# Routing matmuls widened to the full array, capacities added last, and a shorter first routing chain

## The chip, the cores and the metric

The kernel runs on one core of a Trainium2 chip. The metric is device time in microseconds of the core. The engines are named as in the profile: PE (TensorE matmuls; PEld are its weight loads), DVE (VectorE), ACT (ScalarE), POOL (GpSimd) and SP (SyncE, which issues DMAs).

## The reference

Three computations follow each other on 2304 tokens of width 512. Attention with 4 x 8 heads (sequence 576, head width 64) adds a softmax over a sequence averaged by four and a softmax over a band of width 7. A mixture of 8 experts routes each token to one expert with a capacity of 288 tokens, by a greedy walk over all token and expert pairs in order of their gate logit. A feed-forward network (512 to 2048 to 512) with g = h * tanh(softplus(h)) follows.

```python
x = _attn_ref(q, k, v)            # (2304, 512) after the reshape
logits = x @ w_gate               # (2304, 8)
for idx in np.argsort(-logits.flatten()):
    tok, e = idx // 8, idx % 8
    if assigned[tok] >= 0 or counts[e] >= 288: continue
    assigned[tok] = e; counts[e] += 1
for e in range(8):
    out[assigned == e] = np.maximum(x[assigned == e] @ w1[e], 0) @ w2[e]
h = out @ w_in; out = (h * np.tanh(softplus(h))) @ w_out
```

## The kernel before

Attention (class `Attn`, L57 to L310) works on 16 pairs of heads, three groups of three 64-token blocks each, and writes x transposed into `xT`. A list of operations sorted by hand-set keys (`TP`) gives the order in which they are written; a scheduler then orders each engine's queue. `rmm` (L241) multiplies a 128-token tile of `xT` with the identity and the gate weights into the PSUM tile `rp`, in two halves; `rxr` copies the rows out on ACT, `rlg` sums the logits on DVE into `L`, and `rst` stores the rows to DRAM. `rp` has one buffer of tag "rw", and from tile 15 on half of the calls take the one buffer of tag "pd".

The router (class `Router`, `phase` L394) finds in phase k the next expert that fills up, and its 288 tokens. A phase takes the maximum of the remaining logits per token (`m`), a one-hot of its expert (in `AO[:, 1]`, called OH; `AO[:, 0]`, called A, holds the tokens already given away), and an integer key whose digits are searched in five levels. A level (L441) compares a digit with 128 or 64 thresholds (`cmp`, DVE), counts by expert on PE (`cnt`: one matmul with the negative capacities, `nrem`, from one partition, then 18 with 8 weight columns, L455), turns the signs into a count `fl` (`jk`, DVE), sends it to all partitions by a matmul (the vote `j8`, L462, 9 rows), and takes the largest (`jb`). Then `full` marks the expert, `s8` and `sf` (L485 to L487) pick its tokens, two matmuls (`to`, 36 columns, copied to `ts`; and `pp`) number them, and `it` (18 matmuls with 3 weight columns) and `ip` (a transpose) give the index list `idx` for the gather (`gather`, L692, indirect DMAs on POOL's queue).

In phase 0 `busy` (L385) puts matmuls on constants (`idle`, 128 x 512) into the waits of the routing chain.

The order of stages is a list (L849): phases 0 and 1, then experts E0 to E7, then the FFN groups. While expert k runs, `bg()` (L950) steps routing phase k + 2, so that matmuls of the router stand between those of the expert. An expert (`expert`, L703) transposes its gathered rows (`xtp`, L713), multiplies them with w1 (`hp`, L756 in plain f32, two passes per matmul) and with w2 (`ya`). E1 to E5 also convert pieces of the FFN weights on DVE and ACT (`Narrow`). The FFN is `group` (L772).

Of the kernel before, what the change touches and what calls it, by code (L numbers as in the profile page):

```python
# [29 lines left out]
RPD = 15  # L30
# [26 lines left out]
class Attn:  # L57
# [183 lines left out]
    def rmm(self, t, half):  # L241


        rp = self.rp[t, half] = (self.p_pd.tile([128, 2, 136], F32, name="rp", tag="pd") if t >= RPD and (t + half) % 2
                                 else self.p_rw.tile([128, 2, 136], F32, name="rp", tag="rw"))
        for i in range(2):
            self.nc.tensor.matmul(rp[:, i], self.xT[:, 2 * half + i, 128 * (t % 9):128 * (t % 9) + 128], self.a['idg_sb'][:, 2 * half + i], start=True, stop=True)  # L247
# [17 lines left out]
    def emit(self, nar=None, rload=None):  # L265
# [54 lines left out]
def host_route():  # L320
# [7 lines left out]
    tri = np.zeros((128, 164), f)  # L328
    tri[:, 0:128] = np.triu(np.ones((128, 128), f))
    tri[0:36, 128:164] = np.triu(np.ones((36, 36), f), 1)  # L330

    eye = np.concatenate([np.vstack([np.eye(8) * v, np.ones((1, 8))]) for v in EYES], axis=1)
    return dict(rsmall=small, rthr=it.astype(ml_dtypes.bfloat16), rtri=tri.astype(np.float16), reye=eye.astype(np.float16))

class Router:
    def __init__(self, nc, tc, ctx, a):
# [5 lines left out]
        self.tri = c.tile([128, 164], F16, name="rtri")  # L342
# [51 lines left out]
    def phase(self, k):  # L394
# [9 lines left out]
        A, OH = self.AO[:, 0], self.AO[:, 1]  # L404
# [5 lines left out]
        if not last:  # L410
            m0, sg, key, E = F("m0"), F("sg", I32), F("key", I32), P2("E", BF16)
            dg = [F(f"dg{i}", I32) for i in range(len(SH))]

        for c0, c1 in FIRST if k == 0 else [(0, 18)]:
            c = slice(c0, c1)
            V.tensor_reduce(out=m[:, c], in_=L[:, c], op=ALU.max, axis=AX.X)
            if not last:
                V.tensor_scalar_add(m0[:, c], m[:, c], 0.0)
                mi = m0[:, c].bitcast(I32)
# [7 lines left out]
            if k:  # L427
                wm2 = F("wm2")
                V.scalar_tensor_tensor(out=wm2, in0=self.inact, scalar=100.0, in1=wm, op0=ALU.mult, op1=ALU.add)
            V.tensor_tensor(out=OH[:, c], in0=w2[:, c], in1=bc8((wm2 if k else wm)[:, c]), op=ALU.is_equal)  # L430
# [3 lines left out]
        if not last:  # L434
# [6 lines left out]
            for l, K in enumerate(KS):  # L441
# [18 lines left out]
                V.tensor_scalar(out=jk[:, 0:K], in0=cnt[:, 0:K], scalar1=0.0, scalar2=0.0, op0=ALU.is_ge, op1=ALU.add, accum_out=fl[0:8])  # L460
# [14 lines left out]
            V.tensor_scalar(out=full, in0=fw, scalar1=fm[:, 0:1], scalar2=None, op0=ALU.is_equal)  # L475
# [3 lines left out]
        else:  # L479
            V.tensor_scalar(out=full, in0=self.rem, scalar1=30000.0, scalar2=None, op0=ALU.is_lt)  # L480
# [40 lines left out]
        R = sm.tile([128, 18, 3], F16, name="R")  # L521
# [27 lines left out]
        if not last:  # L549
# [8 lines left out]
            V.tensor_tensor(out=A, in0=A, in1=ON, op=ALU.add)  # L558
# [3 lines left out]
            V.tensor_scalar_mul(self.nrem, self.rem[0:1], -1.0)  # L562
# [81 lines left out]
class FFN:  # L644
# [58 lines left out]
    def expert(self, k, rows, exi):  # L703
# [9 lines left out]
        for dc in range(4):  # L713
            t = ps['h'].tile([128, 288], F32, name="xtp", tag="h")
            for g in range(3):
                nc.tensor.transpose(t[:, 96 * g:96 * g + 96], rows[g][:, 128 * dc:128 * dc + 128], self.a['ident_sb'][0:96, 0:96])
            if plain:
                (nc.vector.tensor_copy if dc % 2 else nc.scalar.copy)(xh[:, dc], t)
            else:
                nc.scalar.copy(xh[:, dc], t)  # L720
                nc.vector.tensor_tensor(out=xl[:, dc], in0=t, in1=xh[:, dc].bitcast(F32), op=ALU.subtract)
# [166 lines left out]
def body(nc, tc, a):  # L888
    with ExitStack() as ctx:
# [20 lines left out]
        nar.hold = hold  # L910
        def after(ins):
# [57 lines left out]
```

## Time and profile before

| | |
|---|---|
| Median of three runs | 899.55 us (895.21, 899.55, 899.56) |
| Profiled execution, its span | 894.45 us, 892.7 us |
| PE busy | 868.1 us (97%), 6792 instructions |
| PE weight loads | 728.0 us (82%) |
| DVE busy | 665.1 us (75%), 1819 instructions |
| ACT, POOL busy | 462.4 us (52%), 142.7 us (16%) |
| Mean granted PE clock | 0.998 of full speed (2.4 GHz) |
| Chain that ended last, by engine | PE 74%, DVE 12%, ACT 7%, issue 2%, DMA 2% |

A busy PE is not a PE at its peak: matmuls are pipelined, and a matmul counts as busy until its modelled end, so what a matmul costs is read from the distance between starts. A share over the span mixes stages; the stages are told apart by windows below.

### The profile page before, as it was taken

How to read it: one execution, taken by the hardware profiler on the slowest of the kernel's cores; microseconds unless marked ns; L12 is line 12 of the kernel's file. 1: busy time of each engine (PE TensorE's matmuls, PEld its weight loads, DVE VectorE, ACT ScalarE, POOL GpSimd, SP SyncE). 2: the span in 40 equal slices, each digit the busy share in tenths (PEclk: the TensorE clock that was granted, in tenths of full speed). 3: DMA queues.
4: the chain of work that ended last, by engine and by line, in shares of the span. 5: the costliest groups of instructions: out<-in, count | busy, mean ns of one | idle time of the engine just before them, and what ended most of it. 6: DMA issues, size and time to landing. Idle time of an engine off the chain costs nothing.

```text
span 892.7 us, 18176 instructions
## 1 busy us (share of the span) xinstructions
PE 868.1 (97%) x6792; PEld 728.0 (82%) x6792; DVE 665.1 (75%) x1819; ACT 462.4 (52%) x1136; POOL 142.7 (16%) x203
## 2 busy tenths in 40 slices
PE   7999999999989999999999999999998999999995
PEld 4778876466767777788999999999998999999994
DVE  6999876657879898987664788888887565665655
ACT  4778774012323233244555776666666565555553
POOL 5654410101202010112001000000000011111101
PEclk9999999999999999999999999999999999999999
DMA  8866522335575464659643343433333143333312
GB/s 214 201 193 193 170 91 91 100 110 158 165 227 186 160 221 154 225 181 299 210 148 101 84 119 119 119 118 109 118 95 93 48 118 95 95 96 95 95 48 71
DMA packets 69851, 123.44 MB, mean 138 GB/s; under 512 B 8738, under 2 KB 35618, under 8 KB 69762
## 3 DMA queue, kind: packets, MB, share of 16 engines
q1 hardware_dynamic: 34146, 75.08, 27.0%
q0 software_dynamic: 21984, 28.32, 12.4%
q10 hardware_dynamic: 13632, 18.88, 6.2%
q8 instruction: 53, 0.87, 0.4%
q14 instruction: 36, 0.29, 0.1%
HBM read 98.65 MB, written 23.60 MB: 137 GB/s over the span
## 4 chain that ended last, share of the span: by engine, by line
PE 74%; DVE 12%; ACT 7%; issue 2%; DMA 2%; POOL 1%; SPq 0%; POOLq 0%; DVEq 0%; ACTq 0%
PE hp L756 11%; PE hm L680 5%; PE hm L681 5%; PE hm L679 5%; PE oa L681 5%; PE oa L679 5%; PE oa L680 5%; PE ya L679 4%; PE ya L680 3%; PE ya L681 3%; PE cnt L455 3%; PE ya L730 2%; PE pvl L221 2%; PE sp L181 2%; PE rp L247 2%
## 5 line engine op out<-in xcount | busy, mean ns | idle before, releaser
L679 PE MATMUL hm<-Yh,wM_sb 128*128 128x256 f32 x576 | 161.5, 280 | 2.4 <-issue 2.4
L680 PE MATMUL hm<-Yl,wM_sb 128*128 128x256 f32 x576 | 162.3, 282 | 0.0
L681 PE MATMUL hm<-Yh,wM_sb 128*128 128x256 f32 x576 | 162.3, 282 | 0.0
L756 PE MATMUL hp<-xh,w 128*128 128x288 f32 x384 | 116.0, 422 | 0.0
L679 PE MATMUL oa<-wM_sb,gh 128*128 128x512 f32 x288 | 112.7, 391 | 2.6 <-ACT gh L841 2.6
L679 PEld LDWEIGHTS hm<-Yh,wM_sb 128*128 128x128 f32 x576 | 108.9, 189 | 5.5 <-issue 2.8
L681 PE MATMUL oa<-wM_sb,gl 128*128 128x512 f32 x288 | 113.0, 392 | 0.0
L680 PE MATMUL oa<-wM_sb,gh 128*128 128x512 f32 x288 | 112.3, 390 | 0.0
L680 PEld LDWEIGHTS hm<-Yl,wM_sb 128*128 128x128 f32 x576 | 108.8, 189 | 2.8
L681 PEld LDWEIGHTS hm<-Yh,wM_sb 128*128 128x128 f32 x576 | 108.4, 188 | 0.0
L841 ACT CAST gh<-eu 128x512 fp32r<-128x512 f32 (+1 forms) x73 | 44.9, 615 | 111.0 <-DVE eu L838 111.0
L835 DVE SCALAR_TENSOR_TENSOR eu<-eu 128x512 f32<-128x512 f32 (+1 forms) x73 | 50.1, 686 | 63.6 <-ACT eu L834 63.3
L765 ACT ACTIVATE gh<-hp 128x288 fp32r<-128x288 f32 (+1 forms) x64 | 26.2, 410 | 101.8 <-PE hp L756 87.3
L842 DVE TENSOR_TENSOR gl<-eu,gh 128x512 fp32r<-128x512 f32 (+1 forms) x73 | 50.0, 685 | 36.2 <-ACT gh L841 36.0
L756 PEld LDWEIGHTS hp<-xh,w 128*128 128x128 f32 x384 | 65.5, 189 | 13.0
L679 PE MATMUL ya<-gh,wbh 128*128 128x288 f32 x224 | 73.0, 329 | 0.0
L680 PE MATMUL ya<-gl,wbh 128*128 128x288 f32 x224 | 68.1, 305 | 0.0
L681 PE MATMUL ya<-gh,wbl 128*128 128x288 f32 x224 | 67.4, 302 | 0.0
L832 ACT ACTIVATE eu<-eu,one_sb 128x512 f32<-128x512 f32 (+1 forms) x73 | 52.3, 716 | 27.8 <-DVE eu L831 27.4
L681 PEld LDWEIGHTS oa<-wM_sb,gl 128*128 128x128 f32 x288 | 54.0, 188 | 12.3 <-DVE gl L842 0.8
L679 PEld LDWEIGHTS oa<-wM_sb,gh 128*128 128x128 f32 x288 | 54.1, 188 | 12.2 <-ACT gh L841 3.4
L680 PEld LDWEIGHTS oa<-wM_sb,gh 128*128 128x128 f32 x288 | 54.1, 188 | 9.1
(188 smaller groups left out, 1895.9 us busy)
## 6 DMA issues: line engine op xcount, KB each, us to landing
n<-in_wM_dram SPq DMA_DIRECT2D x32, 512.0 KB
w<-in_wE_dram SPq DMA_DIRECT2D x56, 256.0 KB
w2r<-in_wE_dram SPq DMA_DIRECT2D x40, 256.0 KB
Yh<-y_dram POOLq DMA_DIRECT2D x18, 512.0 KB, 5.7
Yl<-y_dram POOLq DMA_DIRECT2D x18, 512.0 KB, 5.1
wraw<-in_wE_dram SPq DMA_DIRECT2D x16, 512.0 KB
vw<-in_vw_dram SPq DMA_DIRECT2D x16, 315.0 KB
kT<-in_kT_dram SPq DMA_DIRECT2D x16, 291.0 KB
```

The lines of the kernel that those rows point to most:

```text
L181: self.mm = self.nc.tensor.matmul(sp[r, u], q[r, 64 * n:64 * n + 64], k[r, 64 * n:64 * n + W], start=False, stop=u == 2)
L221: self.nc.tensor.matmul(op[c, u], vw[:, 3 * g + u, c], d['aT'][:, u, c], start=True, stop=True)
L455: ct = nc.tensor.matmul(cnt[:, 0:K], OH[:, c, :], cmp[c], start=False, stop=(c == 17))
L679: mm(out, lh, rh, start=first, stop=False)
L680: mm(out, lh, rl, start=False, stop=False)
L681: mm(out, ll, rh, start=False, stop=last)
L756: nc.tensor.matmul(hp, w1[:, 128 * dc:128 * dc + 128], xh[:, dc], start=dc == 0, stop=dc == 3)
L765: self.cast = nc.scalar.activation(out=hh[:, 0:288], in_=hp, func=AF.Relu)
L832: nc.scalar.activation(out=u, in_=e, func=AF.Square, bias=one)
L835: nc.vector.scalar_tensor_tensor(out=u, in0=u, scalar=1.0, in1=r, op0=ALU.add, op1=ALU.mult)
L841: self.cast = nc.scalar.copy(gh[:, 0:w], e)
L842: self.mark = nc.vector.tensor_tensor(out=gl[:, 0:w], in0=e, in1=gh[:, 0:w].bitcast(F32), op=ALU.subtract)
```

## The change

All router matmuls get more than 64 weight columns and more than 64 rows, by zeros around the data (`OHw`, `Rw`, `nrem`, `eyes`, `fl`); only the first 13 counts of phase 0 stay at 8 columns. The capacities are spread over 128 partitions and from phase 1 on added after the counts. The `to` matmul and its copy give way to a running sum on DVE (`run`), and the tokens already given away are kept as one number per token (`aid`), so that `s8`, `sf` and A go. The last two `rp` tiles take PSUM buffers of the attention's scores and transposes. `xtp` holds one gather group with four 96-column pieces instead of one piece of all groups.

```diff
 def rmm(self, t, half):
-        rp = self.rp[t, half] = (self.p_pd.tile(...) if t >= RPD and (t + half) % 2 else self.p_rw.tile(...))
+        pool, tag = (self.p_pd, "pd") if t >= RPD and (t + half) % 2 else (self.p_rw, "rw")
+        if t >= 16:
+            pool, tag = (self.p_sc, "sc") if t == 16 else (self.p_tr, "tr")
...
-                add(k + TP['rlg'], self.rlg, t, h)
+                add(k + (TP['rxr'] - 0.01 if t >= 16 else TP['rlg']), self.rlg, t, h)
...
-    tri[:, 0:128] = np.triu(np.ones((128, 128), f))
-    tri[0:36, 128:164] = np.triu(np.ones((36, 36), f), 1)
-    eye = np.concatenate([np.vstack([np.eye(8) * v, np.ones((1, 8))]) for v in EYES], axis=1)
+    tri = -np.tril(np.ones((128, 128), f), -1)
+    eye = np.concatenate([np.vstack([np.eye(8) * v, np.zeros((64, 8)), np.ones((1, 8))]) for v in EYES], axis=1)
...
-        self.AO = c.tile([128, 2, 18, 8], F16, name="rAO")
+        self.OHw = c.tile([128, 208], F16, name="rOH")
+        self.Rw = [c.tile([128, 123], F16, name=f"rR{i}") for i in range(2)]
+        self.aid = c.tile([128, 18], F32, name="raid")
-        self.nrem = c.tile([1, 8], F16, name="rnrem")
+        self.nrem = c.tile([128, 72], F16, name="rnrem")
...
-                V.tensor_scalar_add(m0[:, c], m[:, c], 0.0)
-                mi = m0[:, c].bitcast(I32)
+                mi = m[:, c].bitcast(I32)
...
-                cnt = self.psr.tile([8, 128], F32, name="cnt", tag="rt")
-                nc.tensor.matmul(cnt[:, 0:K], self.nrem, self.one[0:1, 0:K], start=True, stop=False)
+                cnt = self.psr.tile([72, 128], F32, name="cnt", tag="rt")
+                nr = lambda a, b: nc.tensor.matmul(cnt[:, 0:K], self.nrem, self.one[:, 0:K], start=a, stop=b)
+                if not k:
+                    nr(True, False)
                 for c in range(18):
-                    ct = nc.tensor.matmul(cnt[:, 0:K], OH[:, c, :], cmp[c], start=False, stop=(c == 17))
+                    mm = 8 if not (l or k) and c < FIRST[0][1] else 72
+                    ct = nc.tensor.matmul(cnt[0:mm, 0:K], self.OHw[:, 8 * c:8 * c + mm], cmp[c], start=(k > 0 and c == 0), stop=(k == 0 and c == 17))
+                if k:
+                    nr(False, True)
...
-                jm = nc.tensor.matmul(j8, fl.to_broadcast([9, 128]), self.eye[1 if end else KS[l + 1]], start=True, stop=True)
-                self.busy(k, 16 if end else 4, jm)
+                jm = nc.tensor.matmul(j8, fl.to_broadcast([73, 128]), self.eye[1 if end else KS[l + 1]], start=True, stop=True)
+                self.busy(k, 7 if end else 4, jm)
...
-        V.tensor_tensor(out=s8, in0=self.AO.rearrange("p h c e -> p (h c) e"), in1=row8(full, 36), op=ALU.mult)
-        V.tensor_reduce(out=sf.rearrange("p h c -> p (h c)"), in_=s8, op=ALU.max, axis=AX.X)
-            V.tensor_tensor(out=sel, in0=ge, in1=sf[:, 1:2].to_broadcast([128, 2, 18]), op=ALU.mult)
-            V.tensor_tensor(out=sel[:, 0], in0=sel[:, 0], in1=sf[:, 0], op=ALU.add)
+            V.scalar_tensor_tensor(out=sel, in0=own.unsqueeze(1).to_broadcast([128, 2, 18]), scalar=fm[:, 0:1], in1=ge, op0=ALU.is_equal, op1=ALU.mult)
+        V.scalar_tensor_tensor(out=sel[:, 0], in0=aid, scalar=fm[:, 0:1], in1=sel[:, 0], op0=ALU.is_equal, op1=ALU.add)
-        nc.tensor.matmul(to[0:n], s2, self.one, start=True, stop=True)
-        V.tensor_copy(ts[0:n], to[0:n])
+        V.tensor_tensor_scan(out=run[:, 0:n], data0=self.one[:, 0:n], data1=s2, initial=0.0, op0=ALU.mult, op1=ALU.add)
-        self.busy(k, 9, nc.tensor.matmul(pp[:, 0:n], ts[0:n], self.tri[0:n, 128:128 + n], start=False, stop=True))
+        self.busy(k, 9, nc.tensor.matmul(pp[:, 0:n], self.one, run[:, 0:n], start=False, stop=True))
...
-            nc.tensor.matmul(it, R[:, c, :], oa[c], start=(c == 0), stop=(c == 17))
+            nc.tensor.matmul(it, Rw[:, 3 * c:3 * c + 72], oa[c], start=(c == 0), stop=(c == 17))
-        self.busy(k, 18, nc.tensor.transpose(ip, ig, self.a['ident_sb'][0:3, 0:3]))
+        self.busy(k, 20, nc.tensor.matmul(ip, ig, self.a['ident_sb'][0:72, 0:3], start=True, stop=True))
...
-        for dc in range(4):
-            t = ps['h'].tile([128, 288], F32, name="xtp", tag="h")
-            for g in range(3):
-                nc.tensor.transpose(t[:, 96 * g:96 * g + 96], rows[g][:, 128 * dc:128 * dc + 128], ...)
-                (nc.vector.tensor_copy if dc % 2 else nc.scalar.copy)(xh[:, dc], t)
+        for g in range(3):
+            t = ps['h'].tile([128, 4, 96], F32, name="xtp", tag="h")
+            for dc in range(4):
+                tp = nc.tensor.transpose(t[:, dc], rows[g][:, 128 * dc:128 * dc + 128], ...)
+            if g < 2:
+                self.busy(k, 1 + g, tp)
+                (nc.vector.tensor_copy if g == 1 else nc.scalar.copy)(xh[:, :, q], t)
```

The scheduler writes other queues from this. Three places follow, each before and then changed; line numbers are those of the respective file.

PE at the end of attention, from the last attention output (`pvl`) to the router's first matmul; the numbers tell the `rp` tiles apart. Before:

```order
L221 MATMUL pvl_2800<-aT_2795,vw_2371 64x64 x5
L247 MATMUL rp_2827<-idg_sb_106,xT_105 128x136 [waits DVE_49]
L247 MATMUL rp_2812<-idg_sb_106,xT_105 128x136 [waits DVE_49]
L247 MATMUL rp_2812<-idg_sb_106,xT_105 128x136
L247 MATMUL rp_2827<-idg_sb_106,xT_105 128x136 [waits DVE_49]
L247 MATMUL rp_2820<-idg_sb_106,xT_105 128x136 [waits DVE_49]
L247 MATMUL rp_2820<-idg_sb_106,xT_105 128x136
L247 MATMUL rp_2834<-idg_sb_106,xT_105 128x136 [waits DVE_49]
L247 MATMUL rp_2834<-idg_sb_106,xT_105 128x136
```

Changed:

```order
L221 MATMUL pvl_2809<-aT_2804,vw_2378 64x64 x5
L249 MATMUL rp_2834<-idg_sb_113,xT_112 128x136
L249 MATMUL rp_2841<-idg_sb_113,xT_112 128x136 [waits PE_49]
L249 MATMUL rp_2821<-idg_sb_113,xT_112 128x136 [waits DVE_49]
L249 MATMUL rp_2821<-idg_sb_113,xT_112 128x136
L249 MATMUL rp_2834<-idg_sb_113,xT_112 128x136 [waits DVE_49]
L249 MATMUL rp_2841<-idg_sb_113,xT_112 128x136
L249 MATMUL rp_2827<-idg_sb_113,xT_112 128x136 [waits DVE_49]
L249 MATMUL rp_2827<-idg_sb_113,xT_112 128x136
```

Before, three tiles after the last `pvl` wait for DVE to release a buffer or to fill `xT`, the last being 2834; now 2834 and 2841 have buffers of their own, and of the two tiles that still share one, 2827 ends the list.

DVE in phase 0 after the last vote, from `full` on (`ON` is the one-hot of tokens above the cut, `e` and `exi` give the expert's number, `rinact` the tokens out of play). Before, up to the second `sel`; the copy of `to` and pz follow 8 and 13 rows later:

```order
L475 TENSOR_SCALAR full<-fw,fm 128x8
L504 TENSOR_TENSOR ON<-rAO,ge 128x144
L485 TENSOR_TENSOR s_3162<-rAO,full 128x288
L546 SCALAR_TENSOR_TENSOR e_3258,ex<-full,rsmall 128x8
L552 TENSOR_SCALAR nf<-full 128x8
L487 TENSOR_REDUCE sf<-s_3162 128x36
L548 CAST exi<-ex 1x1
L553 TENSOR_TENSOR L<-L,nf 128x144
L492 TENSOR_TENSOR sel<-ge,sf 128x36
L556 TENSOR_TENSOR rinact<-rinact,ge 128x18
L558 TENSOR_TENSOR rAO<-rAO,ON 128x144
L493 TENSOR_TENSOR sel<-sel,sf 128x18
```

Changed, up to `pz`:

```order
L510 TENSOR_SCALAR full<-fw,fm 128x8
L502 SCALAR_TENSOR_TENSOR sel<-wm,fm,ge 128x36
L513 TENSOR_TENSOR ON<-rOH,ge 128x144
L503 SCALAR_TENSOR_TENSOR sel<-raid,fm,sel 128x18
L556 SCALAR_TENSOR_TENSOR e_3248,ex<-full,rsmall 128x8
L562 TENSOR_SCALAR nf<-full 128x8
L506 SCALAR_TENSOR_TENSOR run<-ones_67,sel 128x36
L558 CAST exi<-ex 1x1
L563 TENSOR_TENSOR L<-L,nf 128x144
L516 TENSOR_TENSOR pz<-sel,pp 128x36
```

The product and maximum over both halves of `rAO` are gone, `run` stands where the path over `to` was, and no row of the next phase stands between `sel` and `pz`.

PE in E0, between two runs of counts of one search level (before phase 1, level 2 to 3). Before:

```order
L455 LDWEIGHTS rAO
L455 MATMUL cnt<-cmp,rAO 8x128
L756 MATMUL hp<-xh,w_3598 128x288
L462 LDWEIGHTS rfl_71
L462 MATMUL j_3369<-reye,rfl_71 128x8
L756 MATMUL hp<-xh,w_3643 128x288
L451 LDWEIGHTS rnrem
L451 MATMUL cnt<-ones_67,rnrem 8x64
L756 MATMUL hp<-xh,w_3643 128x288 x2
L455 LDWEIGHTS rAO
L455 MATMUL cnt<-cmp,rAO 8x64
```

Changed:

```order
L465 LDWEIGHTS rOH
L465 MATMUL cnt<-cmp,rOH 72x128
L458 LDWEIGHTS rnrem
L458 MATMUL cnt<-ones_67,rnrem 72x128
L771 MATMUL hp<-xh,w_3584 128x288
L474 LDWEIGHTS rfl_71
L474 MATMUL j_3359<-reye,rfl_71 128x8
L771 MATMUL hp<-xh,w_3584 128x288
L771 MATMUL hp<-xh,w_3627 128x288 x2
L465 LDWEIGHTS rOH
L465 MATMUL cnt<-cmp,rOH 72x64
```

The capacity matmul (`rnrem`) left its place between the hp matmuls and stands at the end of the counts; the number of hp matmuls between vote and counts is the same.

## Rows read from the trace of the kernel before

**Rows 1.** Table by stages: length, busy of PE, PEld, DVE, ACT, POOL; clock, DMA.
```profile
0.00:146.60 146.60, 140.91 (x1821) 108.97 (x1821) 121.27 (x455) 105.08 (x497) 60.08 (x93) 1.00 0.59 162
...
182.00:224.10 42.10, 42.10 (x296) 27.31 (x295) 28.59 (x112) 6.25 (x13) 3.69 (x7) 1.00 0.43 140
224.10:420.80 196.70, 194.20 (x1410) 152.28 (x1410) 170.09 (x579) 67.83 (x140) 28.90 (x44) 1.00 0.63 201
...
477.70:892.70 415.00, 403.48 (x2593) 366.23 (x2592) 291.05 (x498) 252.78 (x417) 45.70 (x52) 1.00 0.34 99
```

**Rows 2.** Timeline of PE in E0: start, us, what, x instructions.
```profile
185.44 0.17 PE L462 MATMUL j<-reye,rfl 9*128 9x8 f16 x1
185.55 0.75 PE L756 MATMUL hp<-xh,w 128*128 128x288 f32 x2
186.23 0.19 PE L451 MATMUL cnt<-ones,rnrem 1*8 1x64 f16 x1
186.35 1.24 PE L756 MATMUL hp<-xh,w 128*128 128x288 f32 x4
187.51 0.69 PE L455 MATMUL cnt<-cmp,rAO 128*8 128x64 f16 x18
188.13 0.75 PE L756 MATMUL hp<-xh,w 128*128 128x288 f32 x2
188.82 0.17 PE L462 MATMUL j<-reye,rfl 9*128 9x8 f16 x1
```

**Rows 3.** Timeline of PE later in E0.
```profile
200.84 0.23 PE L530 MATMUL cn<-ON,ones 128*128 128x144 f16 x1
200.90 1.67 PE L756 MATMUL hp<-xh,w 128*128 128x288 f32 x6
202.40 0.41 PE L730 MATMUL ya<-gh,w 128*128 128x288 f32 x1
```

**Rows 4.** Timeline of PE in the attention stretch.
```profile
137.69 0.49 PE L207 MATMUL trl<-ident_sb,al 128*70 128x128 f32 x3
138.11 0.47 PE L163 MATMUL opd<-adT,v 72*64 72x144 f32 x4
...
141.85 0.33 PE L221 MATMUL pvl<-aT,vw 70*64 70x64 f32 x2
142.11 0.52 PE L207 MATMUL trl<-ident_sb,al 128*70 128x128 f32 x3
142.47 0.63 PE L247 MATMUL rp<-idg_sb,xT 128*128 128x136 f32 x4
```

**Rows 5.** Groups of PE instructions by line and shape, 182 to 420.8 us.
```profile
L455 PE MATMUL cnt<-cmp,rAO 128*8 128x128 f16 x198 | 12.9, 219 | 0.0
L455 PE MATMUL cnt<-cmp,rAO 128*8 128x64 f16 x324 | 12.4, 193 | 0.0
```

**Rows 6.** Chain that ended last, end of attention: start, us, what.
```profile
148.24 0.74 PE rp L247 x4
...
149.64 0.74 PE rp L247 x4
```

**Rows 7.** Timeline of DVE, end of the first routing chain.
```profile
165.00 0.23 DVE L472 SCALAR_TENSOR_TENSOR fw<-j,jb,rsmall 128x8 f32<-128x8 f32 x1
...
166.36 0.44 DVE L487 TENSOR_REDUCE sf<-s 128x36 f16<-128x288 f16 x1
...
167.00 0.16 DVE L492 TENSOR_TENSOR sel<-ge,sf 128x36 f16<-128x36 f16 x1
...
169.36 0.19 DVE L507 TENSOR_TENSOR pz<-sel,pp 128x36 f32<-128x36 f16 x1
...
174.66 0.14 DVE L543 CAST idx<-ip 96x3 int32<-96x3 f32 x1
```

**Rows 8.** Waits of PE, 224.1 to 420.8 us: total, times, longest.
```profile
PE j L462 <- DVE jk L460: 2.4, 1, 2.4
```

**Rows 9.** Timeline of DVE in E3.
```profile
325.71 0.69 DVE L674 TENSOR_TENSOR wbl<-w2r,wbh 128x512 fp32r<-128x512 f32 x1
```

More of the change, by code (lines that the diff above doesn't have):

```diff
@@ L241, in rmm @@
     def rmm(self, t, half):
-        rp = self.rp[t, half] = (self.p_pd.tile([128, 2, 136], F32, name="rp", tag="pd") if t >= RPD and (t + half) % 2
-                                 else self.p_rw.tile([128, 2, 136], F32, name="rp", tag="rw"))
+        pool, tag = (self.p_pd, "pd") if t >= RPD and (t + half) % 2 else (self.p_rw, "rw")
+        if t >= 16:
+            pool, tag = (self.p_sc, "sc") if t == 16 else (self.p_tr, "tr")
+        rp = self.rp[t, half] = pool.tile([128, 2, 136], F32, name="rp", tag=tag)
         for i in range(2):
@@ L410, in phase @@
         if not last:
-            m0, sg, key, E = F("m0"), F("sg", I32), F("key", I32), P2("E", BF16)
+            sg, key, E = F("sg", I32), F("key", I32), P2("E", BF16)
             dg = [F(f"dg{i}", I32) for i in range(len(SH))]
@@ L427, in phase @@
             if k:
-                wm2 = F("wm2")
-                V.scalar_tensor_tensor(out=wm2, in0=self.inact, scalar=100.0, in1=wm, op0=ALU.mult, op1=ALU.add)
-            V.tensor_tensor(out=OH[:, c], in0=w2[:, c], in1=bc8((wm2 if k else wm)[:, c]), op=ALU.is_equal)
+                own = F("own")
+                V.scalar_tensor_tensor(out=own, in0=self.inact, scalar=-100.0, in1=wm, op0=ALU.mult, op1=ALU.add)
+            else:
+                own = wm
+            V.tensor_tensor(out=OH[:, c], in0=w2[:, c], in1=bc8(own[:, c]), op=ALU.is_equal)
             if not last:
@@ L479, in phase @@
         else:
-            V.tensor_scalar(out=full, in0=self.rem, scalar1=30000.0, scalar2=None, op0=ALU.is_lt)
+            fw = sm.tile([128, 8], F32, name="fw")
+            V.scalar_tensor_tensor(out=fw, in0=self.rem, scalar=30000.0, in1=self.down, op0=ALU.is_lt, op1=ALU.mult)
+            fm = sm.tile([128, 1], F32, name="fm")
+            V.tensor_reduce(out=fm, in_=fw, op=ALU.max, axis=AX.X)
         n = 18 if last else 36
         yield
-        s8 = wk.tile([128, 36, 8], F16, name="s8", tag="s8")
@@ L496, in phase @@
-        nc.tensor.matmul(to[0:n], s2, self.one, start=True, stop=True)
-        ts = sm.tile([36, 128], F16, name="ts")
-        V.tensor_copy(ts[0:n], to[0:n])
+        run = sm.tile([128, 36], F16, name="run")
+        V.tensor_tensor_scan(out=run[:, 0:n], data0=self.one[:, 0:n], data1=s2, initial=0.0, op0=ALU.mult, op1=ALU.add)
         pp = self.psr.tile([128, 36], F32, name="pp", tag="rt")
-        nc.tensor.matmul(pp[:, 0:n], self.tri[:, 0:128], s2, start=True, stop=False)
-        self.busy(k, 9, nc.tensor.matmul(pp[:, 0:n], ts[0:n], self.tri[0:n, 128:128 + n], start=False, stop=True))
+        nc.tensor.matmul(pp[:, 0:n], self.tri, s2, start=True, stop=False)
@@ L502, in phase @@
+        self.busy(k, 9, nc.tensor.matmul(pp[:, 0:n], self.one, run[:, 0:n], start=False, stop=True))
+        V.tensor_scalar(out=full, in0=fw, scalar1=fm[:, 0:1], scalar2=None, op0=ALU.is_equal)
         if not last:
@@ L557, in phase @@
             V.tensor_tensor(out=self.inact, in0=self.inact, in1=tq, op=ALU.add)
-            V.tensor_tensor(out=A, in0=A, in1=ON, op=ALU.add)
+            na = sm.tile([128, 18], F32, name="na")
+            V.scalar_tensor_tensor(out=na, in0=own, scalar=0.0, in1=ge[:, 0], op0=ALU.max, op1=ALU.mult)
+            V.tensor_tensor(out=aid, in0=aid, in1=na, op=ALU.add)
             r1 = sm.tile([128, 8], F32, name="r1")
@@ L712, in expert @@
             xl = self.xs.tile([128, 4, 288], F32R, name="xl")
[L713 to L716 removed]
+        for g in range(3):
+            t = ps['h'].tile([128, 4, 96], F32, name="xtp", tag="h")
+            q = slice(96 * g, 96 * g + 96)
+            for dc in range(4):
+                tp = nc.tensor.transpose(t[:, dc], rows[g][:, 128 * dc:128 * dc + 128], self.a['ident_sb'][0:96, 0:96])
+            if g < 2:
+                self.busy(k, 1 + g, tp)
             if plain:
[L718 removed]
+                (nc.vector.tensor_copy if g == 1 else nc.scalar.copy)(xh[:, :, q], t)
             else:
[L720 to L721 removed]
+                nc.scalar.copy(xh[:, :, q], t)
+                nc.vector.tensor_tensor(out=xl[:, :, q], in0=t, in1=xh[:, :, q].bitcast(F32), op=ALU.subtract)
         st = {}
@@ L910, in body @@
         nar.hold = hold
+        f.busy = r.busy
         def after(ins):
```

37 lines of the change are left out of this document (19 added, 18 removed).

## Prediction

> **What bounds the kernel now.** I read the table by stages first, then the timeline of TensorE inside one stage, then the VectorE timeline of the first routing chain. The stages [rows 1]: attention up to 146.6 us, then (182.0 to 420.8) the experts with the routing of later experts woven in, and from 477.7 on the FFN. In the expert stretches PE is busy for 42.10 of 42.10 us and 194.20 of 196.70 us, so what PE does there is the time. DVE is the next engine: 170.09 of 196.70 us, 86%.
>
> What PE does there is not all work. In the timeline [rows 2] two passes of hp (one f32 matmul is two passes) take 0.75 us busy and four take 1.24, so a pass costs (1.24 - 0.75)/2 = 0.245 us. Between the starts of the vote (j, 185.44) and of the capacity matmul (cnt from rnrem, 186.23) lie 0.79 us with two passes: the vote cost 0.79 - 0.49 = 0.30 us, although it streams 8 columns. The capacity matmul costs 1.28 - 0.98 = 0.30. The 18 counts: 188.82 - 187.51 = 1.31 us with two passes, so 0.82; each is pipelined at (0.69 - 0.193)/17 = 0.029 us (0.193 is the mean of one [rows 5]), in all 0.53, and 0.29 is extra. So each visit of a narrow matmul among wide ones costs about 0.3 us beyond its streaming.
>
> A routing matmul of full shape is there too: cn, 128 rows by 128 columns, 144 columns streamed. From its start to that of the next ya are 200.84 to 202.40 = 1.56 us with six passes (1.47): it costs 0.09, of which 0.06 is its streaming (the next hp starts at 200.90) [rows 3]. So the 0.3 belongs to the shape, and about 0.05 is left at full shape (I take the hp pass as 0.2425 there, from the digits behind these rows; by 0.245 it is 0.03). Where the limit lies, the attention stretch tells [rows 4]: three transposes with 70 weight columns take 0.42 us until a matmul with 64 columns may start (137.69 to 138.11), but 0.36 until one with 128 (142.11 to 142.47), even though the latter run itself followed a 64-column one (141.85). 70 columns count as wide, 64 do not; the change pads to 72 or 73.
>
> **The change, part by part.**
>
> *Visits in the expert stretches.* There are 198 + 324 = 522 counts there [rows 5], at 18 per level 29 levels. Per level: the vote falls from 0.30 to 0.08 (0.05 and 0.03 of streaming), 0.22 saved; the capacity matmul joins the run of counts instead of standing alone, 0.03 is left, 0.27 saved; the counts' extra falls from 0.29 to 0.05, 0.24 saved. That is 0.73 x 29 = 21.2 us. Each of seven phase ends loses `to` (0.3 and its 128 columns, 0.35) and saves 0.24 on each of the second pp, it and ip: 1.07 x 7 = 7.5 us. PE is freed of 28.7 us: 6.9 in E0 (8 levels, one phase end) and 21.8 in E1 to E5. The counts themselves keep their pace: 64 thresholds take 0.029 us with 8 weight columns, and the loads of the next weights are hidden.
> A rule speaks against that. The Trainium skill, TensorE: Matmul & The Clock Gate, section Weight-path perf modes — Fast Weight Load (FWL) and DoubleRow, says that the fast weight load is on only for 128 weights of a type other than FP32; by it 72 fp16 columns load one at a time, an estimate of 30 ns at 2.4 GHz, which no longer hides. By that rule the sum would shrink by some 3 ns x 54 counts x 7 phases = 1.1 us; no row here shows a 72-column fp16 load.
>
> *What holds that back.* DVE has 196.70 - 170.09 = 26.6 us idle in E1 to E5 [rows 1]. The change takes from it per phase the product over both one-hot halves and its maximum, the copy m0, the copy of `to` and one third of an xtp copy, and adds a scan and one small product: about 1.1 us less by the durations of such rows (the maximum alone is 0.44 [rows 7]), some 6 us over the stretch. If PE gained all 21.8, DVE would be idle 26.6 - 21.8 + 6 = 10.8 of 175 us, 94% busy in order, with the routing chain waiting for PE at every level. PE waited for DVE there only once, 2.4 us [rows 8]; it will wait more. I give 4 us back there and 1 us in E0, where between counts and vote one hp pair and about 0.05 us remain of one hp pair and 0.29, so that PE reaches the vote 0.2 us sooner. Bounds: nothing given back, or half of the 21.8. So 28.7 - 5 = 23.7, say 24 us.
>
> *The last rp tiles.* They share one PSUM buffer, and each round of matmul, ScalarE copy and VectorE sum takes 149.64 - 148.24 = 1.40 us [rows 6]. Now tiles 16 and 17 have buffers of their own, and one round instead of two follows the last attention output: 1.4 us saved (0 to 2.8).
>
> *The first routing chain.* From fw to pz took 165.00 to 169.36 = 4.36 us, with the `to` matmul, its copy and queued operations in between; pz to idx (169.36 to 174.66) takes 5.30 [rows 7]. Now 14 instructions lie between fw and pz; ten took 165.00 to 166.36 = 1.36, so about 1.9, and 0.2 for the wait on pp: 2.1, that is 2.2 saved. The scan is not in the trace: between 0.16 (a product of 36 elements) and 0.44 (a maximum over 288) [rows 7]; I take 0.25, nearer the first, since it has 36. The key and one-hot operations of the next phase, which used to fill the waits, now stand behind pz and ct, ahead of idx: 0.4 and about 0.5 us. Net -1.3 (0 to -2.2). The missing m0 hop and the vote's shorter waits give 0.4, the rows transposed by gather group 0.1. With the rp round this chain is 3.2 us shorter (1.5 to 5).
>
> *What costs nothing.* Four more POOL memsets stand at the start, where the first inputs are still being loaded. The scheduler orders the attention stretch anew; its engines get the same work, so I take 0, between -1.5 and +1.5 (1% of 146.6). From the first FFN matmul on, all three compute engines have the same order as before: 415 us untouched [rows 1].
>
> Sum: 24 + 3.2 = 27 us off. The profiled execution took 894.45, hence 867.5. It is 5.1 us under the median of the three runs, 899.55 (the lowest is 895.21); against the median the change gives 872.5. **I predict 872.**
>
> **Rivals.**
> *DVE becomes the bound.* For: 86% busy, in order, and at most 6 us lighter. Against: it waited for PE, not the reverse. Then E1 to E5 give 11 and E0 5, the chain 2: 18 us, 881.
> *The padding does not remove the 0.3 us*, because something else than the width makes it, so that the change does not do what it says. Then only the merged capacity matmuls (29 x 0.27 = 7.8), `to` (7 x 0.35 = 2.5) and the chain (3.2) count: 13.5 us, 886. Against: cn and the 70-column transposes.
> *Slower: votes queue behind DVE's other work.* The 0.3 us visits gave DVE time to answer. Without them PE reaches each vote and each count run early, and what is ahead in DVE's queue, such as a weight split of 0.69 us [rows 9], becomes PE time, 58 times: 40 us against 27 saved, 913. It decides from a mean wait of 27/58 = 0.47 us. Against: PE waited once in 196.70 us [rows 8], and the gap to fill is at most 0.3.
>
> **How the numbers follow.** PE's gain mostly kept: 0.73. DVE the bound: 0.16. Padding without effect: 0.06. Queueing, slower: 0.03. The rest, 0.02, is an attention order that costs several us. The range goes from everything kept, 899.55 - 28.7 - 5 - 1.5, and 2 more because single executions lie up to 5.1 under the median: 862, to the DVE case with 1.5 for the chain and 1.5 for the attention order on top: 884. Two executions of this kernel differ by up to 0.5%, which is also about what a measurement can tell from no change: 4.5 us. Faster by more than that 0.94, within 0.03, slower 0.03.
>
> **What would show it.** In the profile of the changed kernel the vote among hp passes should cost 0.08 us in place of 0.30, and counts should start one hp step after hp. The stretch from the first hp of E0 to the end of E5 should fall from 239 to about 215 us, with PE waits on jk and cmp of 0.05 to 0.2 us at votes. First hp at about 179 us instead of 182. From the first FFN matmul to the end 415 us as before. I am wrong if the vote still costs 0.2 or more, if DVE is above 96% busy while PE idles, or if the attention stretch moves by over 2 us.

## The result, and the profile after

The changed kernel takes 890.54 us (median of 6 runs, 888.76 to 891.47) against 898.21 before (6 runs, 895.02 to 899.56): ratio 0.9916, 95% interval 0.9892 to 0.9939. It is faster by 7.7 us, where 26 to 27 were forecast: 872, with a range of 862 to 884.

The table by stages of the changed kernel, columns as in [rows 1]. Its boundaries are the last rp, the first hp, the first xtp of E1, and that of E6 (left out below: E6 and E7, 57.0 us, as before). The last rp starts at 152.28 us, 150.09 before.

```profile
152.30:182.20 29.90, 25.14 (x228) 14.40 (x226) 19.42 (x103) 1.74 (x5) 3.91 (x7) 1.00 0.43 144
182.20:221.10 38.90, 37.98 (x316) 29.19 (x317) 27.76 (x114) 6.06 (x13) 4.96 (x7) 1.00 0.48 152
221.10:415.80 194.70, 181.42 (x1391) 155.81 (x1390) 163.09 (x562) 67.20 (x140) 35.95 (x44) 0.98 0.62 204
...
472.80:887.70 414.90, 404.87 (x2594) 367.73 (x2592) 290.67 (x498) 253.03 (x417) 45.65 (x52) 0.99 0.34 99
```

E0 takes 38.9 us (42.1 before), E1 to E5 194.70 (196.70), the FFN 414.9 (415.0). In E1 to E5 PE is no longer busy throughout: 181.42 of 194.70. DVE is not busier either: 163.09 us, 84%. Both engines idle more than before.

The padding itself did what it should. PE in E0, as in [rows 2]:

```profile
186.44 0.79 PE L465 MATMUL cnt<-cmp,rOH 128*72 128x64 f16 x18
187.06 0.20 PE L458 MATMUL cnt<-ones,rnrem 128*72 128x64 f16 x1
187.10 0.73 PE L771 MATMUL hp<-xh,w 128*128 128x288 f32 x2
187.67 0.17 PE L474 MATMUL j<-reye,rfl 73*128 73x8 f16 x1
187.70 1.70 PE L771 MATMUL hp<-xh,w 128*128 128x288 f32 x6
189.24 0.79 PE L465 MATMUL cnt<-cmp,rOH 128*72 128x64 f16 x18
```

Counted as in the prediction, with 0.245 us taken off for each hp pass: the vote costs 189.24 - 187.67 - 1.47 = 0.10 us (0.30 before), the capacities 187.67 - 187.06 - 0.49 = 0.12 (0.30), a run of 18 counts 187.06 - 186.44 = 0.62 (0.82). A level costs 0.84 us beside the passes, 1.42 before.

So PE was freed, and then it waited. PE's waits from the start of E1 to the start of E6 (what, for what: total, times, longest):

```profile
PE j L474 <- DVE jk L472: 8.1, 6, 2.0
PE ip L551 <- DVE ig L547: 4.1, 1, 4.1
PE pp L508 <- DVE sel L503: 0.9, 1, 0.9
```

13.1 us, where [rows 8] had 2.4. What jk waits for is seen at the 2.03 us wait in E4. First PE, then DVE, then ScalarE (timelines: start, us, what, and in brackets the idle time before and what ended it):

```profile
359.49 0.29 PE L691 MATMUL ya<-gh,wbh 128*128 128x288 f32 x1
361.82 0.18 PE L474 MATMUL j<-reye,rfl 73*128 73x8 f16 x1 [2.03 <-DVE jk L472]
```

```profile
360.87 0.69 DVE L653 TENSOR_TENSOR wM_sb<-nt,wM_sb 128x512 fp32r<-128x512 f32 x1 [2.13 <-ACT wM_sb L652]
361.48 0.27 DVE L472 TENSOR_SCALAR_CACHE_REDUCE jk<-cnt 8x128 f16<-8x128 f32 x1
```

```profile
359.70 0.62 ACT L685 CAST wbh<-w2r 128x512 fp32r<-128x512 f32 x1 [2.61 <-DMA w2r<-in_wE_dram]
360.23 0.61 ACT L652 CAST wM_sb<-nt 128x512 fp32r<-128x512 f32 x1
360.74 0.40 ACT L780 ACTIVATE gh<-hp 128x288 fp32r<-128x288 f32 x1
```

Read backwards: the vote at 361.82 waits for jk; jk stands on DVE behind the FFN split wM_sb; that waits 2.13 us for its half on ScalarE, which stands there behind wbh; and wbh waits for the load w2r of step 5 to land. That split is not needed for two more steps: on ScalarE it stands ahead of gh of step 4 (360.74). The chain of waits has the same pieces, and the load at their head:

```profile
353.96 5.71 DMA w2r<-in_wE_dram
...
359.70 0.62 ACT wbh L685
360.32 0.53 ACT wM_sb L652
...
360.87 0.69 DVE wM_sb L653
361.56 0.21 DVE jk L472 x2
...
361.82 0.18 PE j L474
```

It took 5.71 us. The other four waits of PE over 1.4 us have a w2r load at the head of their chains too, of 4.42 to 7.85 us; the longest, the 4.1 us for ip:

```profile
390.30 7.85 DMA w2r<-in_wE_dram
...
399.73 0.33 PE ip L551 x2
```

ScalarE waits for such landings 55.6 us in E1 to E5; before, it was 29.6, and hidden:

```profile
ACT wbh L685 <- DMA w2r<-in_wE_dram: 55.6, 27, 5.2
```

```profile
ACT wbh L673 <- DMA w2r<-in_wE_dram: 29.6, 18, 4.0
```

The first of these lines is the changed kernel's, the second that of before. Some of the waits are then paid a second time. The stretch after the vote of E4, by window:

```profile
363.00:366.80 3.80, 3.80 (x13) 2.73 (x12) 3.23 (x7) 0.00 (x0) 0.00 (x0) 0.55 0.37 124
366.80:371.00 4.20, 4.20 (x40) 3.65 (x39) 3.19 (x11) 1.03 (x2) 0.00 (x0) 1.00 0.55 183
```

After the wait PE's granted clock falls to 0.55 of full (1.2 GHz for most of these 3.8 us) while it is busy for all of them. After the 4.1 us for ip it falls too (0.62 from 399.80 to 403.40); after the waits of 1.4 to 1.9 us in E1 and E2 it stays at 1.00.

The first routing chain, to set beside [rows 7]:

```profile
166.72 0.23 DVE L484 SCALAR_TENSOR_TENSOR fw<-j,jb,rsmall 128x8 f32<-128x8 f32 x1
...
168.04 0.23 DVE L506 TENSOR_TENSOR_SCAN run<-ones,sel 128x36 f16<-128x36 f16 x1
...
168.53 0.19 DVE L516 TENSOR_TENSOR pz<-sel,pp 128x36 f32<-128x36 f16 x1
...
174.58 0.14 DVE L553 CAST idx<-ip 96x3 int32<-96x3 f32 x1
```

From fw to pz 1.81 us (4.36 before), the scan 0.23, pz to idx 6.05 (5.30).

### The profile page after: what moved, and what is told of

It is laid out like the page before. It is cut to its first block, busy times and chain, and to the rows that moved or that the text cites. A ratio compares the mean times of both kernels' runs of the same rounds, so it can differ in the third digit from the quotient of the medians.

```text
span 887.7 us, 18153 instructions
## 1 busy us (share of the span) xinstructions
PE 850.8 (96%) x6788; PEld 735.4 (83%) x6788; DVE 658.2 (74%) x1797; ACT 461.5 (52%) x1134; POOL 150.4 (17%) x207
## 4 chain that ended last, share of the span: by engine, by line
PE 36%; DVE 34%; ACT 17%; DMA 7%; issue 4%; SPq 0%; POOL 0%; POOLq 0%; DVEq 0%; ACTq 0%
PE hp L771 6%; DMA w2r<-in_wE_dram 5%; DVE eu L850 5%; DVE eu L851 4%; DVE eu L853 4%; ACT eu L848 4%; ACT eu L847 4%; ACT gh L856 4%; ACT eu L849 3%; DVE gl L857 3%; PE ya L691 2%; PE ya L692 2%; PE pvl L221 2%; PE ya L693 2%; PE sp L181 2%
## 5 line engine op out<-in xcount | busy, mean ns | idle before, releaser
L771 PE MATMUL hp<-xh,w 128*128 128x288 f32 x384 | 109.0, 422 | 0.6 <-ACT xh L733 0.6
L771 PEld LDWEIGHTS hp<-xh,w 128*128 128x128 f32 x384 | 70.0, 194 | 15.1 <-ACT xh L733 0.8
L685 ACT CAST wbh<-w2r 128x512 fp32r<-128x512 f32 x40 | 24.8, 620 | 76.3 <-DMA w2r<-in_wE_dram 64.0
```

Of the source, the lines that this page charges most:

```text
L771: nc.tensor.matmul(hp, w1[:, 128 * dc:128 * dc + 128], xh[:, dc], start=dc == 0, stop=dc == 3)
```

## The experiments

All of them stand against runs of the kernel before on the same chip. "E1 to E5" is from the first xtp of E1 to that of E6, "PE waits" the sum of its waits there (timeline and waits of each profile).

| kernel | median us | ratio, 95% interval | E1 to E5 | PE waits |
|---|---|---|---|---|
| before | 898.21 | | 196.6 | 2.4 |
| changed | 890.54 | 0.9916, 0.9892 to 0.9939 | 194.7 | 13.1 |
| 1 memsets on VectorE | 888.99 | 0.9898, 0.9866 to 0.9930 | 197.7 | 13.3 |
| 2 six w2r buffers | 888.44 | 0.9886, 0.9852 to 0.9920 | 196.3 | 13.8 |
| 3 w2r loaded once | 871.65 | 0.9703, 0.9672 to 0.9734 | 179.2 | 1.3 |
| 4 padding alone | 890.09 | 0.9910, 0.9875 to 0.9945 | 192.6 | 7.6 |
| 5 before, w2r loaded once | 898.17 | 1.0010, 0.9988 to 1.0032 | 196.3 | 1.7 |
| 6 n loaded once | 875.92 | 0.9757, 0.9707 to 0.9808 | 186.0 | 6.7 |
| 7 six buffers, split later | 870.60 | 0.9696, 0.9639 to 0.9754 | 178.8 | 1.1 |
| 8 pieces to E6, E7 | 885.77 | 0.9851, 0.9802 to 0.9901 | 197.9 | 13.1 |
| 9 split later alone | 874.00 | 0.9707, 0.9655 to 0.9759 | 178.0 | 0.6 |
| 10 before, with 7's edits | 907.71 | 1.0091, 1.0059 to 1.0124 | 206.4 | 6.5 |
| 11 = 7, E6's buffers free early | 869.01 | 0.9668, 0.9637 to 0.9699 | 177.5 | 0.3 |
| 12 = 7, 128 columns | 869.62 | 0.9676, 0.9643 to 0.9708 | 177.2 | 0.8 |

**1. Memsets on VectorE.**
```diff
-            nc.gpsimd.memset(t, 0.0)      # OHw, Rw
+            nc.vector.memset(t, 0.0)
```


> The changed kernel with three of its zeroing memsets (OHw and the two Rw tiles) on VectorE in place of POOL; everything else is as in the changed kernel. In the changed kernel POOL's order at the start has the scaling of v (which waits for vd until 12.25 us) ahead of the second q; before, the second q came first. Theory: this swap, brought by the memsets, makes the attention stretch 2 to 3.5 us longer. With the memsets moved the old order is back: the last rp matmul should fall from 152.3 to 149 to 150.5 us and the time from 890.5 to 887 to 888.5, with E1 to E5 (first transposes of E1 to first transposes of E6) unchanged at 194 to 195 us. Rival: the first inputs merely landed later in that run, or the re-scheduled attention as a whole is slower; then the last rp stays at 152 and the time at 890.


The last rp came at 147.85, earlier than expected, and yet this theory falls. Runs 2, 3 and 6 have POOL's order of the changed kernel, and their last rp stands at 148.78, 147.97 and 148.88; run 5, with the attention code of before, has it at 152.85. The 152.28 of the changed kernel belonged to that execution, as the rival said. That E1 to E5 is 3.0 us longer here was not expected: PE waits as long (13.3 us) but is busy 2.8 us longer, 184.25 at a mean clock of 0.97; why the clock fell more often is not known.

**2. Six buffers for w2r.**
```diff
-  raw = self.wa.tile(..., name="w2r", tag="wal")
+  raw = self.wa.tile(..., name="w2r", tag="wal") if j % 2 else self.rawe.tile([128, 1024], F32, name="w2r", tag="wraw")[:, 0:512]
```


> The changed kernel with six buffers in place of three for the raw second expert weights w2r (every other one goes into the pool that only E6 and E7 use). Theory (weight feed): in E1 to E5 a w2r load can be issued only when an old wbl on VectorE has freed its buffer, lands 4 to 8 us later, and wbh on ScalarE, wM_sb behind it, and jk behind that on VectorE all stand in order behind the landing, so that PE waits 13.1 us at votes and ip and loses 3.5 us more to a lower clock. With the loads issued earlier the waits should fall to 2 to 6 us, E1 to E5 from 194.7 to 180 to 188, and the time from 890.5 to 877 to 884. Rival (VectorE's queue): jk stands behind VectorE's own work, whatever lands when; then E1 to E5 stays at 192 to 196 and the time at 889 to 892.


A miss: 888.44 and 196.3. Two waits of this run, of ScalarE and of DVE:

```profile
ACT wbh L685 <- DMA w2r<-in_wE_dram: 63.3, 28, 6.1
```

```profile
DVE gl L783 <- ACT gh L780: 7.9, 4, 5.1
```

ScalarE waits for landings even longer, 63.3 us: the scheduler, seeing free buffers, ordered the splits on ScalarE still earlier (34 of the 40 stand ahead of gh of two steps earlier, 21 in the changed kernel), and now gh, and gl behind it, stand up to 5.1 us. More buffers for the loads don't help while the splits are queued sooner too.

**3. w2r loaded once.**
```diff
+  if raw is None: raw = self.w2c = self.wa.tile(...); nc.sync.dma_start(raw, src[:, 512:1024])
```


> The changed kernel with the raw second weights w2r of E1 to E5 loaded once, for the first step of E1, and that tile split again at each of the 40 steps: 39 loads of 256 KB are left out, the splits on ScalarE and VectorE stay. Theory (weight feed): nothing waits for a landing any more; PE waits in E1 to E5 fall below 4 us, the stretch from 194.7 to 175 to 181 and the time to 870 to 877. Rival (VectorE's queue): same work on VectorE, so 190 to 196 and 887 to 891.


871.65, and in E1 to E5 (window of that stretch):

```profile
216.20:395.40 179.20, 177.67 (x1390) 152.71 (x1389) 163.34 (x561) 66.54 (x138) 28.24 (x44) 1.00 0.53 168
```

DVE does the same 163.34 us of work in 179.20, 91%, and PE is busy for 177.67. So DVE's work was not the bound; waiting for the landings was.

**4. Padding alone.** The kernel before with cnt, vote, it and nrem widened as in the change:
```diff
-  ct = nc.tensor.matmul(cnt[:, 0:K], OH[:, c, :], cmp[c], ...)
+  ct = nc.tensor.matmul(cnt[0:mm, 0:K], self.AOw[:, 144 + 8 * c:144 + 8 * c + mm], cmp[c], ...)   # mm = 72
```


> The kernel before with the padding alone: counts with 72 weight columns, votes with 73 rows, capacities from 128 rows, index counts with 72 columns; the capacities still come first, the sums by to and ts, the rows' transposes and the first chain are as before. PE is relieved of about 0.22 (vote), 0.05 to 0.27 (capacities) and 0.24 (counts) us per level, 29 times, and 0.24 to 0.7 at each phase end: 17 to 21 us in all. Theory (weight feed): E1 to E5 gives nearly all of that back, 196.7 to 190 to 197; E0 42.1 to 38 to 40; the time 892 to 897 against 898 before. Rival (the padding is worth what PE is freed of, and something else in the change costs it): E1 to E5 at 180 to 185, the time 880 to 885.


890.09: as fast as the whole change, and a little under the 892 to 897 of the theory; E1 to E5 came as it said (192.6), E0 a little longer (40.6 for 38 to 40). PE's busy time in E1 to E5 falls by 9.2 us (to 184.97), the stretch by 4.0. Of the five waits of 0.9 us and more there, three have a w2r load of 4.7 to 6.5 us at the head of their chains and one a load of n.

**5. The control for 3.** The same edit on the kernel before.


> The control for the run with w2r loaded once: the kernel before with the same edit (39 loads of 256 KB left out, every split kept). Theory: before, PE set the pace of E1 to E5 and the landings were hidden behind it, so leaving the loads out gives only PE's few waits back: E1 to E5 from 196.6 to 193 to 196.5 us, the time from 898 to 894 to 898. Rival: the weight feed bound the kernel before as well; then E1 to E5 falls by 8 us or more.


898.17, ratio 1.0010. Before, the w2r landings cost nothing that can be told. They became the bound only when PE got faster.

**6. n loaded once.**
```diff
+  if 0 < i < 16: return i, self.rt0...    # no load
```


> The changed kernel with the raw FFN weights n of the first 16 pieces loaded once: 15 loads of 512 KB are left out of E0 to E5, all splits of them on ScalarE and VectorE stay. If the share of the DMA engines that n takes makes w2r land late, w2r lands within about 3 us of its issue, PE's 13.1 us of waits fall by half or more, E1 to E5 goes from 194.7 to 180 to 187 and the time to 876 to 883. If w2r is late because it is issued late (its buffer is freed by a wbl that VectorE reaches 10 us and more after the data are there, or SP stands before another load), E1 to E5 stays at 190 to 196 and the time at 886 to 891.


875.92 and 186.0, PE's waits halved: the times of the first branch, but not its condition. At the head of three of PE's four longest waits w2r still takes 4.0 to 6.0 us to land, not 3; ScalarE still waits 65.7 us for w2r, and only its 15.4 us of waits for n (nz) are gone. That speaks for the queueing behind n rather than the DMA engines' share, but this run does not tell them apart for certain.

**7. Six buffers, and the split later.** The memsets of 1, the buffers of 2, and:
```diff
-  w2 = self.split(raw, self.wb, "wb")              # ahead of hp's matmuls
+  w2 = self.split(raw, self.wb, "wb", self.cast)   # after gh; the copy wbh is ordered behind gh of its step
```


> The changed kernel with the three memsets on VectorE, six w2r buffers, and the split wbh of step j ordered on ScalarE behind gh of the same step (in the changed kernel wbh of step j stood ahead of gh of step j-1, so everything behind it on ScalarE and VectorE waited for a landing that was not needed for two more steps). Theory: a late landing now holds up nothing but its own split. PE waits in E1 to E5 fall to 2 to 6 us, the stretch to 180 to 187 and the time to 871 to 879. Rival (what binds is the transfers' total, not where the queues stand): E1 to E5 stays at 192 to 198 and the time at 886 to 890.


870.60: as expected, with every load in place. E1 to E5:

```profile
217.20:395.90 178.70, 177.46 (x1390) 153.45 (x1389) 161.66 (x555) 63.38 (x138) 32.76 (x44) 1.00 0.66 216
```

The DMA engines move 216 GB/s there, more than the 204 of the changed kernel, and PE waits for 1.1 us in all. The transfers' total was not the bound.

**8. Pieces moved to E6 and E7.**
```diff
-ORDER = ('R0 R1 E0/3 E1/3 E2/3 E3/3 E4/3 E5/1 E6 E7 ...
+ORDER = ('R0 R1 E0/3 E1/2 E2/2 E3/2 E4/2 E5/1 E6/2 E7/2 ...
```


> The changed kernel with the three memsets on VectorE and four of the FFN weight pieces moved out of E1 to E4 (one each) into E6 and E7 (two each), where VectorE is 57% and the DMA engines 47% busy. Per piece E1 to E4 loses 512 KB of loads and about 4 us of VectorE work. Theory (weight feed): E1 to E5 falls from 195 to 198 us to 184 to 190; E6 and E7 (57.0) grow by 0 to 3; the time 877 to 884. Rival: the waits stay, since w2r still comes late where three splits follow each other: 888 to 890.


E1 to E5 stays at 197.9: the rival. The profiled execution, 889.22, is the longest of four, though; the median, 885.77, lies between the two branches. In the profile less work for DVE (152.98 us) and fewer loads do not help: the splits stand no later than they stood (27 of the 40 ahead of gh of two steps earlier), and PE waits 13.1 us as in the changed kernel.

**9. The split later, alone**: as 7, with three buffers.


> The run with six buffers and the later split, but with the three w2r buffers of the changed kernel: only the order on ScalarE (wbh of step j behind gh of step j) and the three memsets differ from the changed kernel. If the order of the queues alone made PE wait, E1 to E5 falls to 177 to 183 us and the time to 869 to 874, as with six buffers. If the loads must also be issued earlier, a later split frees its buffer later too: E1 to E5 at 186 to 196, the time 880 to 890. I hold the second for likelier.


My likelier branch fell. The order is enough: E1 to E5 takes 178.0 us, and on ScalarE no split of w2r waits for its load (E2 of this run; the split starts right behind gh):

```profile
289.87 0.41 ACT L782 ACTIVATE gh<-hp 128x288 fp32r<-128x288 f32 x1 [3.52 <-PE hp L773]
290.18 0.61 ACT L685 CAST wbh<-w2r 128x512 fp32r<-128x512 f32 x1
```

Its median stands 3.4 us over that of run 7, with runs from 868.65 to 877.30; the profiled one lost its time in the attention stretch (last section).

**10. The control for 7**: its buffers and its split on the kernel before.


> The control: the kernel before with the six w2r buffers and the later split, and nothing of the change. Theory: PE set its pace in E1 to E5, so the weight feed gives it nothing: E1 to E5 at 193 to 197 us, the time within 3 us of before. The whole change is then worth what this run and the run with six buffers and the later split differ by, 24 to 28 us. Rival: the better feed is a gain of its own, whatever PE does: 8 us or more off.


Neither: 907.71, slower by 0.6 to 1.2%. The chain of waits in E1 of this run:

```profile
249.18 6.36 DMA n<-in_wM_dram
...
255.56 0.69 ACT nz L632
...
260.20 0.60 DVE wbl L676
...
261.40 0.38 DVE gl L772
...
261.82 0.61 PE ya L682
262.43 0.24 PE ya L683
```

Here gl stands on DVE behind the FFN split and a wbl. The load of n at the head took 6.36 us, and ScalarE stood idle for the last 2.04 of them; ya waits 2.42 us for gl, then runs at half clock (0.24 us a pass, 0.13 at full clock). The next three waits of ya, 1.03 us each, have no load at their head: gl stands behind DVE's own split work. So the order that helps the changed kernel costs this one 9.8 us in E1 to E5. The trace shows these waits and the fallen clock as the price; why DVE's order costs more at this pace of PE is not traced, and I have not tried a third order on this kernel.

**11. E6's buffers free early.**
```diff
-  tag="wal") if j % 2 else ...
+  tag="wal") if j % 2 or k == 5 and j > 3 else ...
```


> The run with six buffers and the later split, where E6 and E7 took 59.3 us in place of 57.0 because the first weights of E6 waited for buffers that w2r of E5 still held: here the steps 4 to 7 of E5 use the old three buffers alone. E6 and E7 should go back to 57.0 to 57.5, E5 may lose up to 1 us, the time 868.5 to 870.5; if E5 waits for its loads instead, 871 to 873.


869.01; E6 and E7 take 57.6 in place of 59.3. It beats both kernels, with the whole computation.

**12. 128 columns.** nrem, cnt, it and the slices of OHw and Rw with 128 in place of 72.


> The run with six buffers and the later split, with counts, capacities and index counts of 128 weight columns in place of 72. In the changed kernel counts of 64 thresholds follow each other at 0.035 us with 72 columns, where 0.029 was measured before with 8. If the load of 72 columns sets that pace and one of 128 columns is quicker, the counts of 64 thresholds go at 0.027 to 0.030 us, those of 128 thresholds stay at 0.056; E0 to E5 is 1.5 to 2.5 us shorter. If the load's time grows with the columns, 0.05 or more and 5 us longer. If the columns do not matter, 0.035 and no change.


PE's timeline in E2, first of run 7, then of this run:

```profile
284.64 0.79 PE L465 MATMUL cnt<-cmp,rOH 128*72 128x64 f16 x18
285.26 0.20 PE L458 MATMUL cnt<-ones,rnrem 128*72 128x64 f16 x1
```

```profile
284.66 0.70 PE L465 MATMUL cnt<-cmp,rOH 128*128 128x64 f16 x18
285.19 0.19 PE L458 MATMUL cnt<-ones,rnrem 128*128 128x64 f16 x1
```

18 counts of 64 thresholds take 285.26 - 284.64 = 0.62 us with 72 columns and 285.19 - 284.66 = 0.53 with 128. With 18 such levels that is 1.6 us, and E0 to E5 is 1.5 shorter (215.2 against 216.7); the two times cannot be told apart.

## Why the prediction was wrong

**Right in kind, too large in size: what PE is freed of.** "So the 0.3 belongs to the shape", and 72 columns count as wide: the vote went from 0.30 to 0.10, with 0.08 forecast. (That 64 columns are narrow rested on a difference of 0.06 us in [rows 4], and no run tries it.) But a level lost 0.58 us, not 0.73, since the capacities still cost 0.12 and the counts 0.62: about 4 us less over 29 levels. With the landings out of the way (run 9) PE's busy time in E1 to E5 falls by 16.9 us (194.20 to 177.26), where 21.8 were worked out; the rest of the difference is not traced. The stretch falls by 18.6 us, 196.6 to 178.0, since PE's few waits of before go too. That the working had 17.8 there (21.8 less 4) is luck: nothing is given back in run 9. E0 was oversized: 3.2 to 4.1 us gained (38.9 to 38.0) for 5.9. Part of that is moved work: E0 now holds 316 PE instructions, 296 before.

**Right: the first chain.** From the last rp to the first hp 29.9 us against 31.9, 2.0 gained for 1.8 forecast: fw to pz 1.81 (2.1 worked out), the scan 0.23 (0.25), pz to idx 0.75 longer (0.9). The rp round: from the last pvl to the last rp 2.5 us, 3.7 before, 1.2 for 1.4. The attention ahead of that began its last pvl 3.4 us later in this one profile, past the 2 us that the prediction named as a sign of being wrong; the other profiles show that this comes and goes.

**Too small: the wider weights.** The prediction held that the counts keep their pace, and left 1.1 us for wider weights out of the sum. Runs 7 and 12 show that they do not: 0.62 us a run with 72 fp16 columns, 0.53 with 128, as the 0.53 worked out for 8 before. Over 18 such runs the change loses 1.6 us, part of the 4 us above. The Trainium skill (TensorE: Matmul & The Clock Gate, Weight-path perf modes — Fast Weight Load (FWL) and DoubleRow) says that the fast weight load is on for 128 weights that are not FP32; these two runs agree.

**The step that failed: "What holds that back".** I asked only how busy DVE would be (94%), and gave back 4 us in E1 to E5. About 16 of the 18 to 19 us went: the stretch is 16.7 us longer than in run 9, of which 12.5 are PE's waits (13.1 against 0.6) and 4.2 its busy time (181.42 against 177.26), most of it the two falls of the clock. DVE was 84% busy and idle together with PE: a busy share does not tell when an engine's input arrives. What held PE back was w2r landing late, ahead of the votes in queues that run in order: jk stood behind wM_sb, wM_sb behind wbh, wbh behind a load. The working did not hold a single DMA of that stretch, though the trace of before had ScalarE waiting 29.6 us for w2r, in 18 waits, and though the one wait of PE that it did read, 2.4 us for jk [rows 8], has a load at the head of its chain:

```profile
242.85 7.40 DMA n<-in_wM_dram
...
252.25 0.17 PE j L462
```

The waits for w2r were hidden as long as PE needed 196.6 us. In the changed kernel the scheduler also ordered the splits earlier on ScalarE. Counted in the timelines, 21 of the 40 stand ahead of gh of two steps earlier (16 before), and every one ahead of gh of at least one step earlier; before, 8 stood behind that. Padding with an order nearly that of before (run 4) still gave back 5.2 of the 9.2 us, so PE's faster pace alone is enough to meet the landings.

**The rivals.** "The padding does not remove the 0.3 us" came nearest with 886, by a wrong mechanism: the vote fell to 0.10. "DVE becomes the bound", 881, had a wrong one too: run 3 has DVE 91% busy and PE nearly without waits (1.3 us). The slower case, "votes queue behind DVE's other work", named the queue in which jk stands, but charged 58 short delays; there were 8 long ones, of up to 4.1 us.

**The parts and their sum.** Attention +3.4, rp round -1.2, chain -2.0, E0 -3.2, E1 to E5 -2.0, the rest 0: -5.0 us, from 892.7 to 887.7. Forecast were 0, -1.4, -1.8, -5.9, -17.8.

## What to carry to other kernels

Before an engine is made faster in a stretch that it bounds, list what every other engine of that stretch waits for, DMA landings above all: such a wait can cost nothing before the change and be the bound after it, and no busy share shows it. In an in-order queue put an instruction that waits for a load behind the ones that others need sooner; here that one line of order was worth 16 us in the changed kernel, and more buffers without it nothing that could be told. Then check the order again: the one that suits the changed kernel made the kernel before slower (run 10, with six buffers).

## What was not expected of the hardware

A short idle time of PE can be followed by a fall of its clock that costs several times as much. In the profile of run 9, in the attention stretch, PE waits 1.10 us for VectorE (until 54.44 us) and 1.11 us for ScalarE (until 62.20), then:

```profile
60.00:62.00 2.00, 1.08 (x11) 0.81 (x9) 1.91 (x6) 1.22 (x7) 0.71 (x1) 1.00 0.48 146
62.00:64.00 2.00, 1.80 (x26) 1.49 (x26) 1.84 (x5) 1.98 (x11) 0.00 (x0) 0.83 0.00 1
64.00:66.00 2.00, 2.00 (x16) 1.44 (x13) 1.24 (x7) 0.85 (x3) 0.00 (x0) 0.50 0.89 247
...
72.00:74.00 2.00, 2.00 (x20) 1.37 (x19) 1.04 (x3) 0.00 (x0) 1.03 (x3) 0.50 0.01 4
```

From 64 to 74 us it is busy all the time at half clock (0.50, 1.2 GHz), and the last rp comes at 155.42, 7.5 us later than in run 8. In the changed kernel's E4 one wait of 2.03 us was followed by a shorter drop, 363.00 to 366.80. Yet the wait of 2.39 us in the kernel before, longer than any of these three, is followed by none:

```profile
252.25:256.00 3.75, 3.75 (x20) 2.99 (x21) 3.75 (x10) 0.95 (x3) 0.00 (x0) 1.00 0.40 144
```

The Trainium skill (TensorE: Matmul & The Clock Gate, HAM oscillation — how this bites in real kernels) says that PE waiting for a transfer is throttled again. These rows agree in part: the wait in E4 has a load at the head of its chain and was followed by a drop, the one of before has one too and was not, and the two in attention were not for a transfer. Nothing tried here provokes the drop in attention or keeps it away, and what decides whether a wait is followed by one is not shown.
